# Attention and two expert layers in float32: the first layer's low product moved to GpSimd, the second layer's weights joined during the first layer

## Chip, cores and metric

One core of one Trainium2 chip runs the whole program. The metric is the device time of one execution in microseconds. The kernel before was run three times: 968.38, 967.47 and 964.55 us, median 967.47 us. Most executions of one kernel agree within 0.3%.

## The reference

Three steps follow one another. All inputs arrive as float64 words and the output is float32.

```python
# window attention: batch 4, heads 8, sequence 576, head size 64
scores = scale * q @ k.T + bias            # causal, window of 128, one slope for each head
attn = softmax(scores);  x = (attn @ v) as [2304 tokens, 512]
# first layer: rational activation
h = x @ w_in                               # 512 -> 2048
P = a0 + a1*h + a2*h**2 + a3*h**3;  Q = 1 + |b0|*|h| + |b1|*h**2
x = (P / (Q + 1e-6)) @ w_out               # 2048 -> 512
# second layer: ELU
h = x @ w_in2;  g = where(h > 0, h, exp(min(h, 0)) - 1);  out = g @ w_out2
```

## The kernel before

**Two parts of every operand.** A float32 value is split into a high part that TensorE multiplies exactly and a low part that is the rest. A product is three passes, `PASS` = high by high, low by high, high by low (line 229). So each split costs a copy of the high part, mostly on ScalarE, and a subtraction for the low part, mostly on VectorE.

**Weights arrive as float64.** A weight is two 32-bit words. A scale turns the high word into a float32 (`conv_scale`, line 126), a shift brings down the top bits of the low word (`conv_shift`, line 136), an or and a sign join them (`conv_or`, `conv_sign`), and then `conv_hi` and `conv_lo` split the result. `conv_step` (line 173) moves three weights through these stages at once; in the attention the list `STEPS` places the same stages by hand, one letter each (`s`, `a`, `b`, `c`, `h`, `l`).

**Three stages of the program.** In the attention 16 units of one batch and one pair of heads run in a pipeline whose order is `STEPS`; `normalise` runs on GpSimd. The first layer works on six blocks of 384 tokens. Each block has 16 chunks of 128 hidden columns, 96 chunks in all. For chunk `s` the loop at the end of `experts` issues `gemm1(s)` (12 matmuls, line 248), then `gemm2_T(s - 3)` (12 matmuls, line 691), then `rational(s)`, which holds the activation of chunk `s` and the last operations of chunk `s - 1`. At the end of a block `split_x` splits the next block's input into `xs`. The second layer has 24 steps `q`, eight pairs of hidden chunks for three pairs of token blocks. Each multiplies by a scheme of seven products (`product`, line 887) and then by the second weights (`gemm2`, line 903). The products need sums of weight blocks (`sum_w`, line 830, four operations on GpSimd) and of token blocks (`sum_x`, line 866). A planner, `in_order`, sorts all operations of the second layer by assumed costs and due times.

**Where the second layer's weights are joined.** `load_half`, `join_scale` and `join_words` join 20 of its 32 weights during blocks 1 to 4 of the first layer, in halves of 128x256, and store them in DRAM (`joined`). This happens in ten chunks of each block, 40 halves. The other 12 weights, all of the second matrix, are joined in the second layer by `scale_wo` (ScalarE) and `join_wo` (VectorE, lines 138, 145 and 152).

**Around the change.** Each engine has one queue and works in order. VectorE's order in `rational` is `hi` (line 286), `qq` (288), the join, `qq0` (298), `oo*h` (302), the subtraction (304), the sum (306) and `lo` (308). ScalarE's are the square, `qq`, `oo`, `ee` (lines 273 to 278) and the logarithm and exponential that give the reciprocal `rr` (292, 293). In the last block `prepare` makes the sums and splits for the second layer's first step. `h` lies in PSUM in one of four banks; `h2`, `qq`, `oo`, `ee`, `rr`, `ghi` and `glo` lie in SBUF.

## Time and profile before

| What | us |
|---|---|
| Median of three runs | 967.47 |
| The profiled execution, its own time | 965.85 |
| Its span, first to last instruction | 963.8 |
| TensorE busy (matmul) | 927.3 |
| VectorE busy | 864.8 |
| ScalarE busy | 750.6 |
| GpSimd busy | 232.7 |

The span is 2.05 us shorter than the execution's own time, and that execution lies 1.62 us below the median. Matmuls overlap in the record: one lasts about twice the distance from its start to the next one's start, so TensorE counts as busy when its matmuls follow one another. The attention takes the first 150 us or so, the first layer lasts to about 555 us, and the second layer fills the rest. The mean granted clock of TensorE over the span is 0.991 of 2.4 GHz.

### The profile page before, as it was taken

What the parts mean: (1) busy time and instruction counts of PE and PEld (TensorE: products, weight loads), DVE (VectorE), ACT (ScalarE), POOL (GpSimd) and SP (SyncE); (2) the same over time, 40 slices, a digit from 0 to 9 for tenths busy, and PEclk for the clock granted to TensorE, in tenths of its full rate; (3) what the DMA queues carried; (4) which work ended last, traced back from release to release, by engine and by line L of the source; (5) the groups of instructions that cost most, each with busy time, mean ns of one, the idle gap of its engine ahead of it and who ended that gap; (6) DMA issues with size and microseconds to landing.
All of it is one profiled execution on the core that took longest, in us unless ns stands there. A gap on an engine that the chain in (4) does not pass through costs nothing.

```text
span 963.8 us, 16615 instructions
## 1 busy us (share of the span) xinstructions
PE 927.3 (96%) x5494; PEld 842.7 (87%) x5494; DVE 864.8 (90%) x1949; ACT 750.6 (78%) x1628; POOL 232.7 (24%) x296
## 2 busy tenths in 40 slices
PE   7999999999999999999999979899989999999998
PEld 4776668999999999999999978788978989989897
DVE  5999989999999999999999999999988768887753
ACT  5999999889889888888887967666866657766553
POOL 4777764110000000000000152332254221133100
PEclk9999999999999999999999979999999999999999
DMA  6899842001221212211100124243332221322101
GB/s 169 213 236 247 218 131 82 1 23 33 67 66 50 67 50 66 66 50 60 62 28 1 56 69 129 98 140 113 99 121 86 57 77 56 103 94 78 55 1 66
DMA packets 102486, 83.92 MB, mean 87 GB/s; under 512 B 61696, under 2 KB 83200, under 8 KB 102400
## 3 DMA queue, kind: packets, MB, share of 16 engines
q1 hardware_dynamic: 102400, 82.87, 29.7%
q8 instruction: 43, 0.70, 0.3%
q14 instruction: 43, 0.35, 0.1%
HBM read 69.73 MB, written 13.11 MB: 86 GB/s over the span
## 4 chain that ended last, share of the span: by engine, by line
PE 56%; DVE 20%; ACT 13%; issue 7%; SPq 2%; DMA 1%; DVEq 0%; ACTq 0%
PE acc L691 15%; PE h L248 14%; PE acc L903 14%; PE m L887 12%; ACT pT L427 2%; ACT pr_wo L501 2%; ACT pr_wi L501 2%; DVE qq L288 2%; DVE ghi L286 2%; DVE qq L298 2%; DVE op_wo L847 1%; DVE op_wi L847 1%; DVE oo L302 1%; SPq L334 1%; DVE ee L943 1%
## 5 line engine op out<-in xcount | busy, mean ns | idle before, releaser
L248 PE MATMUL h<-xs,w_wi 128*128 128x384 f32 x1152 | 218.1, 335 | 3.9 <-DVE xs L224 3.4
L248 PEld LDWEIGHTS h<-xs,w_wi 128*128 128x128 f32 x1152 | 200.5, 188 | 6.8 <-DVE xs L224 5.3
L691 PE MATMUL acc<-ghi,w_wo 128*128 128x384 f32 x768 | 196.2, 336 | 0.0
L830 POOL TENSOR_TENSOR s<-two_wo 128x256 f32<-128x256 f32 x32 | 33.3, 1041 | 503.5 <-DMA two_wo<-joined_wi 379.6
L691 PEld LDWEIGHTS acc<-ghi,w_wo 128*128 128x128 f32 x768 | 139.8, 189 | 0.0
L691 PE MATMUL acc<-glo,w_wo 128*128 128x384 f32 x384 | 129.6, 338 | 1.8 <-DVE glo L308 1.8
L887 PE MATMUL m<-xo_wo,op_wi 128*128 128x384 f32 x336 | 79.1, 343 | 12.1 <-DVE ee L943 4.8
L903 PE MATMUL acc<-op_wo,ghi 128*128 128x512 f32 x288 | 89.6, 392 | 0.0
L292 ACT ACTIVATE rr<-qq,c_q 128x384 f32<-128x384 f32 x96 | 59.0, 614 | 27.6 <-DVE qq L288 23.7
L887 PEld LDWEIGHTS m<-xo_wo,op_wi 128*128 128x128 f32 x336 | 60.9, 191 | 20.2 <-DVE ee L943 6.4
L887 PE MATMUL m<-xo_wi,op_wi 128*128 128x384 f32 x336 | 78.2, 341 | 0.0
L691 PEld LDWEIGHTS acc<-glo,w_wo 128*128 128x128 f32 x384 | 72.7, 189 | 3.4 <-DVE glo L308 3.3
L274 ACT ACTIVATE qq<-h,b_abs 128x384 f32<-128x384 f32 x96 | 55.4, 577 | 23.8 <-DVE ee L304 23.8
L275 ACT ACTIVATE oo<-h,a_sb 128x384 f32<-128x384 f32 x96 | 68.0, 708 | 0.7 <-DVE ee L306 0.5
L278 ACT ACTIVATE ee<-h,a_sb 128x384 f32<-128x384 f32 x96 | 67.1, 699 | 0.5 <-DVE glo L308 0.5
L288 DVE SCALAR_TENSOR_TENSOR qq<-h,b_abs,qq 128x384 f32<-128x384 f32 x96 | 60.9, 635 | 5.6 <-ACT qq L274 5.6
L949 ACT ACTIVATE oo<-qq 128x384 f32<-128x384 f32 x24 | 12.6, 525 | 64.7 <-DVE qq L943 64.7
L887 PEld LDWEIGHTS m<-xo_wi,op_wi 128*128 128x128 f32 x336 | 61.4, 190 | 0.0
L903 PEld LDWEIGHTS acc<-op_wo,ghi 128*128 128x128 f32 x288 | 53.5, 188 | 8.9
L903 PE MATMUL acc<-op_wo,glo 128*128 128x512 f32 x144 | 57.0, 396 | 0.0
L943 DVE TENSOR_TENSOR ee<-ee,m 128x384 f32<-128x384 f32 x96 | 52.4, 545 | 4.2 <-PE m L887 4.2
L306 DVE TENSOR_TENSOR ee<-ee,oo 128x384 f32<-128x384 f32 x96 | 54.5, 568 | 0.2
(196 smaller groups left out, 2279.5 us busy)
## 6 DMA issues: line engine op xcount, KB each, us to landing
raw_wo<-in_moe_w_out_dram SPq DMA_DIRECT2D x25, 512.0 KB, 4.8
pair<-joined_wo SPq DMA_DIRECT2D x36, 256.0 KB, 2.7
raw_wi<-in_moe_w_in_dram SPq DMA_DIRECT2D x16, 512.0 KB, 4.3
half<-in_moe_w_in_dram SPq DMA_DIRECT2D x32, 256.0 KB, 2.8
two_wo<-joined_wi SPq DMA_DIRECT2D x32, 256.0 KB, 2.9
v<-in_v_dram SPq DMA_DIRECT2D x32, 128.0 KB, 3.0
joined_wi<-whole SPq DMA_DIRECT2D x32, 128.0 KB, 1.8
two_wi<-joined_wi SPq DMA_DIRECT2D x16, 256.0 KB, 3.0
```

The lines of the kernel that those rows point to most:

```text
L248: nc.tensor.matmul(h, lhsT=WT["wi", f][:, SEL[wp], kk * P:(kk + 1) * P], rhs=x[xp][kk], start=(kk == 0 and n == 0), stop=(kk == KD - 1 and ...
L274: nc.scalar.activation(out=qq, in_=h, func=AF.Abs, scale=b_abs[:, 0:1])
L275: nc.scalar.activation(out=oo, in_=h2, func=AF.Identity, scale=a_sb[:, 3:4], bias=a_sb[:, 1:2])
L278: nc.scalar.activation(out=ee, in_=h2, func=AF.Identity, scale=a_sb[:, 2:3], bias=a_sb[:, 0:1])
L288: nc.vector.scalar_tensor_tensor(out=qq, in0=h2, scalar=b_abs[:, 1:2], in1=qq, op0=ALU.mult, op1=ALU.add)
L292: nc.scalar.activation(out=rr, in_=qq, func=AF.Ln, bias=c_q)
L306: nc.vector.tensor_tensor(out=ee, in0=ee, in1=oo, op=ALU.add)
L501: nc.scalar.activation(out=probs(u, n), in_=probs(u, n), func=AF.Exp, scale=-1.0, bias=mx[:, n:n + 1], accum_out=sm[:, n:n + 1],)
L691: nc.tensor.matmul(acc_t[d], lhsT=WT["wo", f][:, SEL[wp], d * P:(d + 1) * P], rhs=gt[SEL[xp]], start=(f == 0 and n == 0), stop=(f == KF - ...
L887: nc.tensor.matmul(out, lhsT=w[:, SEL[wp], c0:c0 + P], rhs=XO[q // NP2, nm, k][:, SEL[xp]], start=(k == 0 and n == 0), stop=(k == 1 and n ...
L903: nc.tensor.matmul(acc_t[T, t], lhsT=gt[SEL[xp]][:, t * P:(t + 1) * P], rhs=w[:, SEL[wp]], start=(first and n == 0), stop=(last and n == 2),)
L943: nc.vector.tensor_tensor(out=t, in0=R[q, x], in1=M[q, m], op=ALU.add)
```

## The change

Five things change.

1. `top_bits` replaces the shift by a GpSimd operation: it reads the low word as an unsigned number, multiplies by 0.994 times two to the minus 29, subtracts 0.455 and lets the conversion to an integer round. It is used in the attention (`a0`, `a1`), in `conv_step`, and in `join_scale`. In `conv_step` the shift comes one stage earlier, the or, the sign and the low part can be put off into the next `rational`, and the low part goes from GpSimd to VectorE.
2. In `rational`, from chunk 4 on, `h2` lies in PSUM (bank 6), so `gemm1` uses three banks for `h` instead of four. `oo*h` is written over `h` in PSUM and the sum reads it there. The last operation, `low`, goes to GpSimd for chunks over 4. VectorE's order is now `hi`, a first put-off operation, `qq0`, a second one, `qq`, the subtraction, `oo*h`, the sum.
3. 30 of the 32 weights are joined in the first layer, 60 halves in 60 chunks (15 of each of blocks 1 to 4), with scale and shift on GpSimd and or and sign on VectorE.
4. In the last block the preparation is spread, two VectorE operations to a chunk, and takes in one more product's operands (`t1`). The first sums of weights of step 1 go to VectorE. The sums of tokens for the next pair of blocks wait for the products of four later steps, one each.
5. The sums of weights of steps 0 to 7 are stored in DRAM and loaded in steps 8 to 23 instead of being made again.

```diff
+    def top_bits(low):
+        nc.gpsimd.tensor_scalar(
+            out=low, in0=low.bitcast(U32), scalar1=0.994 * 2.0 ** -29, scalar2=-0.455,
+            op0=ALU.mult, op1=ALU.add,
+        )
     def conv_shift(key):
-        low, _ = words(key)
-        nc.vector.tensor_scalar(
-            out=low, in0=low, scalar1=29, scalar2=None, op0=ALU.logical_shift_right
-        )
+        top_bits(words(key)[0])
...
         if new:
             conv_scale(new)
+            conv_shift(new)
         if scaled:
-            conv_shift(scaled)
-            conv_or(scaled)
-            conv_sign(scaled)
+            put_off.append(lambda: conv_or(scaled))
+            put_off.append(lambda: conv_sign(scaled))
         if whole:
-            conv_lo(whole)
+            put_off.append(lambda: conv_lo(whole, "D"))
+        while put_off and not later:
+            go_on()
...
-            h2 = row("h2")
+            h2 = bank(6, [P, TB], "h2") if c > 3 else row("h2")
...
+        one, two = beside or (None, None)
         if old:
...
             nc.vector.tensor_tensor(out=hi, in0=ee0, in1=rr0, op=ALU.mult)
+        if one:
+            one()
+        if old:
+            nc.vector.scalar_tensor_tensor(
+                out=qq0, in0=qq0, scalar=EPSC, in1=hi.bitcast(F32), op0=ALU.add, op1=ALU.mult
+            )
+        if two:
+            two()
         if new:
             nc.vector.scalar_tensor_tensor(
                 out=qq, in0=h2, scalar=b_abs[:, 1:2], in1=qq, op0=ALU.mult, op1=ALU.add
...
         if old:
             nc.vector.tensor_tensor(out=ee0, in0=ee0, in1=qq0, op=ALU.subtract)
+            (nc.gpsimd if c > 4 else nc.vector).tensor_tensor(out=low, in0=ee0, in1=rr0, op=ALU.mult)
         if new:
-            nc.vector.tensor_tensor(out=ee, in0=ee, in1=oo, op=ALU.add)
-        if old:
-            nc.vector.tensor_tensor(out=lo, in0=ee0, in1=rr0, op=ALU.mult)
+            nc.vector.tensor_tensor(out=h, in0=oo, in1=h, op=ALU.mult)
+            nc.vector.tensor_tensor(out=ee, in0=ee, in1=h, op=ALU.add)
...
-        early_ones = [("wi", KF + f) for f in range(KF)] + [("wo", KF + 2 * p) for p in range(4)]
+        early_ones = [("wi", KF + f) for f in range(KF)] + [("wo", KF + f) for f in range(KF - 2)]
...
-            nc.scalar.activation(out=w, in_=high.bitcast(F32), func=AF.Copy, scale=2.0 ** -112)
+            nc.gpsimd.tensor_scalar(
+                out=w, in0=high.bitcast(F32), scalar1=2.0 ** -112, scalar2=1.0, op0=ALU.mult, op1=ALU.mult
+            )
+            top_bits(half[n].rearrange("p (c t) -> p c t", t=2)[:, :, 0])
...
-                step((w, "sum"), "POOL", 2900, lambda: sum_w(w), (w, "load"), (w - 1, "lo", "C"), (w - 1, "lo", "D"))
+                if w >= NP2:
+                    step((w, "sum"), "SP", 1200, lambda: load_sums(w), *gone)
+                else:
+                    eng, cost, at = (nc.vector, 1400, "DVE") if w == 1 else (nc.gpsimd, 3500, "POOL")
+                    step((w, "sum"), at, cost, lambda: sum_w(w, eng), (w, "load"), *gone, (w - 1, "kept"))
+                    step((w, "kept"), "SP", 1200, lambda: keep_sums(w), (w, "sum"))
...
-                step(("sum", J, n), "POOL", 2300, lambda n=n: sum_x(J, n), *used, *[("sum", J, i) for i in range(n)])
+                step(("sum", J, n), "POOL", 2300, lambda n=n: sum_x(J, n), *used, (q - 4 + n, "b11"),
+                     *[("sum", J, i) for i in range(n)])
...
-                run_all(gemm1(s, f, x1[j], 4 + s % 4))
+                run_all(gemm1(s, f, x1[j], (4, 5, 7)[(s - 4) % 3]))
...
+            if s >= LAST:
+                prepare(s)
+            elif s >= KF and f < KF - 1 and nj < 2 * len(early_ones):
+                rational(s, beside=(lambda: join_words(nj), lambda: join_sign(nj)))
```

`keep_sums` issues two stores of 256 KB and `load_sums` two loads of 256 KB.

## Rows read from the trace of the kernel before

**Rows 1.** Busy time by stretch: us, then PE, PEld, DVE, ACT, POOL, clock, DMA, GB/s.
```profile
25.00:128.00 103.00, 98.70 (x990) 73.22 (x988) 101.18 (x395) 102.76 (x324) 78.15 (x120) 1.00 0.87 216
128.00:162.00 34.00, 29.97 (x269) 24.20 (x268) 30.54 (x82) 31.98 (x84) 21.00 (x29) 0.95 0.45 137
162.00:222.00 60.00, 58.53 (x334) 57.34 (x333) 59.45 (x116) 50.78 (x98) 8.01 (x4) 1.00 0.03 10
222.00:537.00 315.00, 312.12 (x1795) 310.76 (x1795) 306.70 (x676) 271.93 (x530) 0.00 (x0) 1.00 0.17 51
...
555.00:575.00 20.00, 14.33 (x58) 13.19 (x58) 19.72 (x30) 11.86 (x24) 11.62 (x10) 0.74 0.11 37
575.00:713.00 138.00, 129.26 (x634) 113.73 (x633) 130.07 (x226) 94.24 (x187) 46.84 (x44) 1.00 0.35 113
713.00:964.00 251.00, 247.30 (x1222) 221.04 (x1220) 184.70 (x332) 157.58 (x314) 50.21 (x52) 1.00 0.23 72
```

**Rows 2.** Waits of TensorE from 128 us on: total us, times, longest us.
```profile
PE m L887 <- DVE ee L943: 6.8, 5, 2.4
PE m L887 <- ACT qq L937: 3.7, 1, 3.7
PE h L248 <- DVE xs L224: 3.4, 5, 0.8
PE m L887 <- DVE qq L943: 3.3, 4, 1.6
PE ps_pT L534 <- ACT pT L427: 3.2, 3, 2.0
PE acc L691 <- DVE glo L308: 1.8, 4, 0.8
```

**Rows 3.** Timeline of TensorE inside the first layer: start, us, what.
```profile
301.27 2.24 PE L248 MATMUL h<-xs,w_wi 128*128 128x384 f32 x12
303.35 0.51 PE L691 MATMUL acc<-ghi,w_wo 128*128 128x384 f32 x2
```

**Rows 4.** Timeline of VectorE, one chunk with a join.
```profile
306.10 0.55 DVE L286 TENSOR_TENSOR ghi<-ee,rr 128x384 fp32r<-128x384 f32 x1
...
307.10 0.28 DVE L764 TENSOR_SCALAR half<-half 128x256 int32<-128x256 int32 x1
...
308.22 0.55 DVE L298 SCALAR_TENSOR_TENSOR qq<-qq,ghi 128x384 f32<-128x384 f32 x1
...
310.56 0.55 DVE L286 TENSOR_TENSOR ghi<-ee,rr 128x384 fp32r<-128x384 f32 x1
```

**Rows 5.** Timelines of GpSimd and VectorE where the second layer begins.
```profile
556.30 7.70 POOL L866 TENSOR_TENSOR xT<-xT 128x384 f32<-128x384 f32 x6
...
560.53 1.35 DVE L298 SCALAR_TENSOR_TENSOR qq<-qq,ghi 128x384 f32<-128x384 f32 x1
```

**Rows 6.** Single lines of the second layer, VectorE: count, min/median/max ns, first and last start.
```profile
L943 DVE TENSOR_TENSOR ee<-ee,m x96: 536/546/555, 571.8 to 950.1; 128x384 f32<-128x384 f32 x96
...
L958 DVE SCALAR_TENSOR_TENSOR oo<-oo,ee x24: 541/557/1101, 585.0 to 951.9; 128x384 f32<-128x384 f32 x24
```

**Rows 7.** Timeline of GpSimd, operations that ran undisturbed.
```profile
24.59 0.47 POOL L518 TENSOR_SCALAR pr_wi<-pr_wi,qq 128x256 f32<-128x256 f32 x1
...
578.07 0.73 POOL L830 TENSOR_TENSOR s<-two_wo 128x256 f32<-128x256 f32 x1 [5.30 <-DVE op_wo L847]
```

**Rows 8.** Timelines of GpSimd and VectorE in one unit of the attention.
```profile
107.47 0.94 POOL L518 TENSOR_SCALAR rr<-rr,qq 128x192 f32<-128x192 f32 x1
107.51 0.69 DVE L152 SCALAR_TENSOR_TENSOR cvt<-raw_wo,cvt 128x512 int32<-128x512 int32 x1
109.55 0.78 POOL L130 TENSOR_SCALAR cvt<-raw_wi 128x512 f32<-128x512 f32 x1 [1.15 <-DVE w_wo L166]
```

**Rows 9.** Joins of second-layer weights on VectorE, count, min/median/max ns, first and last start.
```profile
L138 DVE TENSOR_SCALAR raw_wo<-raw_wo x9: 409/418/423, 587.8 to 673.5; 128x512 int32<-128x512 int32 x9
L145 DVE SCALAR_TENSOR_TENSOR pair<-pair,raw_wo x9: 691/693/696, 588.2 to 674.0; 128x512 int32<-128x512 int32 x9
```

149 lines of the change are left out of this document (86 added, 63 removed).

## The prediction

> **What bounds the kernel now.** I read the busy time by stretch first [rows 1]. TensorE is busy for 312.12 of 315 us in blocks 1 to 5 of the first layer and for 247.30 of 251 us after 713 us. A busy TensorE need not be at its peak, so the timeline decides: 12 matmuls take 303.35 - 301.27 = 2.08 us, 0.173 us each [rows 3], and this distance holds through the stage. The change takes no matmul away. So it can only win what TensorE loses in waits and at the lower clock.
>
> The waits say where that is [rows 2]. After the attention there are 19 of them with 6.8 + 3.7 + 3.4 + 3.3 + 1.8 = 19.0 us. A matmul's record lasts 0.34 us while the next one starts after 0.17 [rows 3], so each wait costs about 0.17 more than its idle time: 22.2 us. Every one but the 3.7 ends with a VectorE operation; that one ends with a ScalarE copy into a buffer that VectorE's subtraction of the last chunks has to free first. In the turn to the second layer, 555 to 575 us, the granted clock is 0.74 on average, so about 10.4 of 20 us ran at 1.2 GHz after TensorE had stood idle; TensorE was busy 14.33/20 = 72% of the time, and half of 7.5 us, 3.7 us, is lost. Around the turn from the attention, 128 to 162 us, three waits cost 3.2 + 0.5 us and the clock of 0.95 costs up to 1.7 us. In all 31 us are within reach, which gives a floor near 935.
>
> VectorE is the engine behind them: 101.18 of 103, 306.70 of 315 and 130.07 of 138 us busy in the attention, the first layer and the early second layer [rows 1]. After 713 us it is busy for 184.70 of 251 us, and TensorE waits for nothing worth a row. So the second layer has no stall where VectorE has a quarter of its time free.
>
> **First layer, VectorE and GpSimd.** A chunk with a join takes VectorE 310.56 - 306.10 = 4.46 us: 1.00 for `hi` and `qq`, 1.12 for three word operations, 2.34 for five more at 0.47 [rows 4]. TensorE needs 24 x 0.173 = 4.16. Ten of sixteen chunks have a join, so the mean is 3.34 + 0.70 = 4.04. Afterwards 15 chunks of a block have one, with 1.00 + two thirds of 1.12 (0.75) + four at 0.47 (1.88) + 0.08, since the sum now depends on the operation just before it and starts at its end, 0.55 rather than 0.47. That is 3.71 us. 0.45 us a chunk is free.
>
> GpSimd gets three operations a chunk. The low product has 384 columns; 256 took 0.73 undisturbed [rows 7], so 1.1. Scale and shift have 256 columns each, 0.47 by the nearest row of one input [rows 7]. The sum is 2.04 of 4.16 us, so GpSimd itself doesn't bind. But the two engines disturb each other. Where GpSimd ran six operations back to back, 1.28 us apart, each VectorE operation with two SBUF inputs took 1.35 us instead of 0.55 [rows 5]. The operations that read one operand from PSUM never grew: 96 sums lie between 536 and 555 ns, while those with two SBUF inputs reach 1101 [rows 6]. After the change three of VectorE's eight operations of a chunk read PSUM: `qq` (0.53 of the 1.00), `oo*h` (0.55) and the sum (0.47).
>
> Now the chunk in order. The subtraction releases the low product; `oo*h` and the sum, 1.02 us, run beside its 1.1, so the next `hi` waits 0.08. Scale and shift follow in GpSimd's queue, and they meet `hi`, an or, `qq0` and a sign, all with two SBUF inputs. A one-input operation that met such a VectorE operation ended 0.21 us after it (107.47 + 0.94 against 107.51 + 0.69), so it needs the shared path for less than half of its time alone [rows 8]. Two such meetings cost 0.42 when neither falls beside `qq`, and 0.21 when one does. So VectorE's chunk takes 3.71 + 0.08 + 0.21 to 0.42 = 4.0 to 4.21 us. Against 4.16 that is nothing, or 0.05 x 60 = 3 us. I take nothing, and keep 3 for the range.
>
> The rounding shift reads an unsigned integer, which no row shows. From below it costs what the scale costs, 0.47; from above I take the two-input operation, 0.73 [rows 7]. The 0.26 more would fall beside `qq` or the subtraction, and at worst 60 x 0.26 = 16 us would come on top. I take the lower end, since the nearest row has the same shape and number of inputs.
>
> Other waits that this adds: the scale waits for the store of the half that used its buffer, and the low product stands behind it in GpSimd's queue. `gemm2_T` reads that low part two chunks later, 8.3 us, against 2.04 us of GpSimd's work, so no loss. ScalarE loses a scale; its `ee` now waits for the low product, which ends before ScalarE needs it. Three banks for `h` instead of four still leave 12.5 us until reuse. One store and one load of a half a chunk instead of in two of three go on SP's queue; the DMA engines were busy 17% of the time there [rows 1].
>
> VectorE's backlog at the block ends shrinks: the five waits for `xs`, 3.4 + 0.8 us, lose 2. The four for `glo`, 1.8 + 0.7 us, belong to conversions and preparation on a full VectorE and to GpSimd at the turn; they lose 1.5. In the last block two extra operations a chunk bring VectorE to about 2.96 + 1.0 to 1.2, about the pace of TensorE, so I give no more.
>
> **The turn to the second layer.** GpSimd's 7.70 us of token sums [rows 5] lengthen the last chunks' operations on VectorE by about 0.8 us each. The change moves these sums to later steps, and the first sums of weights go to VectorE. The copy that TensorE awaits comes some 6 us earlier. The waits of 3.7, 1.6 and 0.3 with their 0.5, and 3.7 for the clock, 9.8 in all, lose 7.5. The rest I leave, because VectorE has two chunks' work still to do when the first product starts.
>
> **Early second layer.** From 575 to 713 us eight waits take 8.5 us (6.8, and 3.3 less 1.6) + 1.4. Ten of twelve joins leave. Each is a shift of 0.42, an or of 0.69 [rows 9] and a sign of 0.69 [rows 8], 18 us of VectorE's 130 us, and brings its share to 112 of 138, or 81%, near the 74% at which nothing waits. These waits lose 8.5 of 9.9. The sums kept in DRAM take 16 x 4 operations from GpSimd, but at a time when TensorE waits for nothing, so I cost them at nothing; the two loads a step stand in SP's queue beside DMA engines busy for 23% [rows 1].
>
> **Attention.** ScalarE is busy for 102.76 of 103 us [rows 1], so VectorE's two shifts less a unit win nothing. GpSimd takes two shifts of 0.78, the price of the strided scale of 512 columns. It stood idle 1.15 us right where they come [rows 8], and (103 - 78.15)/12 = 2.07 us in each of some 12 units [rows 1], against 1.56. In the turn to the first layer VectorE loses shifts of 0.42 [rows 9] and gains low parts of 512 columns, about as long as an or, but GpSimd's low parts, which could block it, go. I take a gain of 1, between -4 and 3.
>
> **The sum.** 1 + 2 + 1.5 + 7.5 + 8.5 = 20.5, with 0.5 for the short restarts behind a wait 21 us. The profiled execution took 965.85 us, so 945; it lies 1.6 us below the median, which I don't add.
>
> **A rule against it.** GpSimd's 1.28 us a turn and VectorE's 1.35 [rows 5] show strict turns, while the 0.21 us [rows 8] shows a shorter hold. The Trainium skill, SBUF — State Buffer, section "SBUF: two separate sides", says that the port pair is locked for a whole instruction by whichever starts first and that the other blocks fully. By that rule 1.35 us agrees, but the 0.21 doesn't show a hold of the whole instruction. What such a hold would do here is the second rival.
>
> **The rivals.**
> 1. The turn stays a stall. VectorE at TensorE's pace in the last block arrives late, `h11` comes after the third product is due, and the clock falls as before; then 7.5 + 1.5 is not won, and 954 results. For it: VectorE is as full there as before. Against: the blocked operations go.
> 2. GpSimd holds the path for its whole time, and the engines take turns. Scale and shift then cost VectorE 0.47 each on top: 3.71 + 0.08 + 0.94 = 4.73 us, 0.57 over TensorE, 60 x 0.57 = 34 us: 979, slower than before. It begins to cost at 0.45 us uncovered a chunk and eats the whole gain at 0.80. A shift of twice its price would do the same. For it: strict turns [rows 5]. Against: the short hold [rows 8].
> 3. GpSimd becomes the attention's bound. With shifts of 1.3 us it would work 2.6 - 2.07 = 0.5 us past its slack in each of 12 units: 6 us, 951.
> 4. The change doesn't do what it says: the joins don't fit and VectorE is relieved in name only. 60 halves fit 60 chunks exactly, so this is unlikely; 965.
>
> **How the numbers follow.** The forecast, 945, has 0.66 (936 to 953); rival 1 has 0.14, rival 2 0.11, rival 3 0.05, rival 4 0.04. The range 936 to 960 takes in the forecast, rivals 1 and 3 and the bounds of the unknown costs. Under 0.5% (about what a measurement of this kernel can tell from no change, 963 to 972) lies rival 4 with the upper edge of rival 1, 0.05; slower has rival 2, 0.11; faster the rest, 0.84.
>
> **What would show it.** Right: matmuls 0.173 us apart all through the first layer, VectorE's operations on PSUM still at 0.55 beside GpSimd's, no clock below 0.95 near 560 us, and no waits for `ee` between 575 and 713. Wrong: waits for `glo` or `h` in blocks 1 to 4 (rival 2), a wait of over 3 us at the third product (rival 1), or GpSimd without gaps in the attention and ScalarE below 0.95 there (rival 3).

## The result and the profile after

| | us |
|---|---|
| Kernel before, median (964.55 to 968.38) | 967.5 |
| Changed kernel, median (976.50 to 980.43) | 978.7 |
| Ratio, with its 95% interval | 1.012, 1.009 to 1.015 |
| Profiled execution of the changed kernel, its own time | 979.0 |
| Its span | 977.3 |

The change made the kernel 1.2% slower. The prediction was 945, faster. The two spans differ by 977.3 - 963.8 = 13.5 us, and the first product of each stage in the two traces tells where they come from:

| Stretch | before, us | after, us | difference |
|---|---|---|---|
| Start to the first `gemm2_T` | 162.61 | 163.27 | +0.7 |
| From there to the first product of block 1 | 53.55 | 55.32 | +1.8 |
| Blocks 1 to 4 | 270.15 | 290.14 | +20.0 |
| Block 5, to the second layer's first product | 68.86 | 68.48 | -0.4 |
| Steps 0 and 1 of the second layer | 41.69 | 38.05 | -3.6 |
| Step 2 to the end | 366.9 | 362.0 | -4.9 |

The second layer won 8.5 us, and blocks 1 to 4, where the joins are, lost 20. Busy time by stretch, with the columns of [rows 1]:

```profile
25.00:128.00 103.00, 94.74 (x979) 72.24 (x977) 96.63 (x366) 101.85 (x319) 97.16 (x141) 1.00 0.86 214
...
218.00:509.00 291.00, 281.21 (x1537) 269.88 (x1538) 270.24 (x522) 214.84 (x420) 142.91 (x185) 0.98 0.26 79
...
577.00:598.00 21.00, 14.36 (x82) 13.74 (x81) 19.88 (x38) 15.00 (x32) 6.43 (x7) 0.92 0.25 89
```

In the second row no engine but TensorE looks full: VectorE is busy for 270 of 291 us, GpSimd for half. Before, VectorE had 306.70 of 315 us there [rows 1]. A stage has become slower although its fullest engine after TensorE became emptier, so I looked for the loss in the order and in the waits. The waits of TensorE from 128 us on, to be laid beside [rows 2]:

```profile
PE h L265 <- ACT xs L240: 10.8, 6, 2.4
PE m L926 <- DVE ee L982: 9.6, 5, 6.5
```

The second row's 6.5 us lie in step 1 of the second layer. Of the first row, five belong to the block ends, 1.7 to 2.4 us each, and behind four of them the granted clock stands at 1.2 GHz for 3.4 us. One chunk with a join in the middle of block 2, VectorE first, GpSimd below (start, us, what; the answer to [rows 4]):

```profile
299.70 0.60 DVE L318 SCALAR_TENSOR_TENSOR qq<-h,b_abs,qq 128x384 f32<-128x384 f32 x1
300.23 0.54 DVE L326 TENSOR_TENSOR ee<-ee,qq 128x384 f32<-128x384 f32 x1
300.69 0.55 DVE L329 TENSOR_TENSOR h<-oo,h 128x384 f32<-128x384 f32 x1
301.34 0.55 DVE L330 TENSOR_TENSOR ee<-ee,h 128x384 f32<-128x384 f32 x1
302.03 0.56 DVE L308 TENSOR_TENSOR ghi<-ee,rr 128x384 fp32r<-128x384 f32 x1
302.50 0.64 DVE L786 SCALAR_TENSOR_TENSOR h<-h,half 128x256 int32<-128x256 int32 x1
303.07 0.77 DVE L312 SCALAR_TENSOR_TENSOR qq<-qq,ghi 128x384 f32<-128x384 f32 x1
303.76 0.41 DVE L794 SCALAR_TENSOR_TENSOR h<-half,h 128x256 int32<-128x256 int32 x1
304.10 0.60 DVE L318 SCALAR_TENSOR_TENSOR qq<-h,b_abs,qq 128x384 f32<-128x384 f32 x1
```
```profile
300.94 1.03 POOL L327 TENSOR_TENSOR glo<-ee,rr 128x384 fp32r<-128x384 f32 x1 [1.91 <-ACT rr L322]
302.05 0.82 POOL L778 TENSOR_SCALAR gwhole<-half 128x256 f32<-128x256 f32 x1
302.95 0.48 POOL L141 TENSOR_SCALAR half<-half 128x256 int32<-128x256 uint32 x1
```

VectorE comes round in 304.10 - 299.70 = 4.40 us, without a wait that the view names, against TensorE's 4.16. Read the distance from each start to the next. Three are longer than their operations need: `hi` starts 0.69 us after the sum, and 0.06 after the low product has ended at 301.97; the or takes 0.57 beside the scale; `qq0` takes 0.69 beside the shift. From this I concluded that each of GpSimd's three operations costs VectorE about 0.22 us. That was the first theory, T.

T is right for the scale and the shift and wrong for the low product. `hi` reads `ee`, which is the result of the sum just before it, and it starts 0.69 us after the sum in e3 too, where GpSimd makes no low product (e1, e3 and e11 are edits told below). e3, VectorE first, GpSimd below:

```profile
311.16 0.56 DVE L330 TENSOR_TENSOR ee<-ee,h 128x384 f32<-128x384 f32 x1
311.85 0.56 DVE L308 TENSOR_TENSOR ghi<-ee,rr 128x384 fp32r<-128x384 f32 x1
```
```profile
310.96 0.42 POOL L778 TENSOR_SCALAR h<-half 128x256 f32<-128x256 f32 x1 [3.57 <-DMA joined_wi<-h]
311.46 0.42 POOL L141 TENSOR_SCALAR half<-half 128x256 int32<-128x256 uint32 x1
```

The median of 76 such pairs in e3 is 0.69 us, as in the changed kernel. In two of e1's 78 pairs `hi` started before the low product had ended, once by 0.22 us, and 0.69 us after its sum all the same. In e11, where `hi` belongs to another chunk than the sum before it and doesn't read its result, the distance is 0.47. So the 0.22 us is the price of reading the result of the operation just before, and of GpSimd's three operations two push VectorE, by 0.23 and 0.22 us.

The block end shows something else. ScalarE there, in the changed kernel and then in the kernel before:

```profile
288.57 0.67 ACT L297 ACTIVATE ee<-h,a_sb 128x384 f32<-128x384 f32 x1
290.47 0.61 ACT L322 ACTIVATE rr<-qq,c_q 128x384 f32<-128x384 f32 x1 [1.23 <-DVE qq L318]
...
291.54 1.75 ACT L240 ACTIVATE xs<-xT 128x384 fp32r<-128x384 f32 x4
```
```profile
280.12 0.70 ACT L278 ACTIVATE ee<-h,a_sb 128x384 f32<-128x384 f32 x1
280.91 0.62 ACT L292 ACTIVATE rr<-qq,c_q 128x384 f32<-128x384 f32 x1
...
281.99 1.75 ACT L223 ACTIVATE xs<-xT 128x384 fp32r<-128x384 f32 x4
```

Before, the logarithm follows `ee` at once. After, it waits 1.23 us for `qq`, since VectorE does `qq` only behind `hi`, the or, `qq0` and the sign. The copies of `xs`, for which TensorE stands idle, queue behind it: that was the second theory, O (order).

### The profile page after: what moved, and what is told of

Its sections match the earlier page's. It is cut to its first block, busy times and chain, and to the rows that moved or that the text cites. A ratio compares the mean times of both kernels' runs of the same rounds, so it can differ in the third digit from the quotient of the medians.

```text
span 977.3 us, 16858 instructions
## 1 busy us (share of the span) xinstructions
PE 935.4 (96%) x5494; PEld 845.9 (87%) x5494; DVE 829.9 (85%) x1805; ACT 720.7 (74%) x1578; POOL 357.1 (37%) x466
## 4 chain that ended last, share of the span: by engine, by line
PE 46%; DVE 35%; ACT 10%; issue 5%; POOL 1%; SPq 1%; DMA 1%; DVEq 0%; POOLq 0%; ACTq 0%
PE acc L942 18%; PE m L926 16%; PE h L265 6%; PE acc L713 5%; DVE qq L312 4%; DVE qq L318 4%; DVE ee L330 3%; DVE ee L326 3%; DVE h L329 3%; DVE ghi L308 2%; DVE cvt L152 2%; DVE cvt L159 1%; DVE gwhole L786 1%; DVE h L786 1%; ACT pr_wi L523 1%
## 5 line engine op out<-in xcount | busy, mean ns | idle before, releaser
L265 PE MATMUL h<-xs,w_wi 128*128 128x384 f32 x1152 | 223.7, 342 | 11.0 <-ACT xs L240 10.8
L265 PEld LDWEIGHTS h<-xs,w_wi 128*128 128x128 f32 x1152 | 204.7, 192 | 15.1 <-ACT xs L240 12.7
L327 POOL TENSOR_TENSOR glo<-ee,rr 128x384 fp32r<-128x384 f32 x92 | 93.6, 1017 | 243.5 <-DVE ee L326 146.5
L713 PE MATMUL acc<-glo,w_wo 128*128 128x384 f32 x384 | 132.7, 346 | 0.8 <-DVE glo L327 0.5
L318 DVE SCALAR_TENSOR_TENSOR qq<-h,b_abs,qq 128x384 f32<-128x384 f32 x96 | 58.4, 608 | 9.5 <-ACT ee L297 9.3
L312 DVE SCALAR_TENSOR_TENSOR qq<-qq,ghi 128x384 f32<-128x384 f32 x96 | 65.0, 677 | 0.5
L297 ACT ACTIVATE ee<-h,a_sb 128x384 f32<-128x384 f32 x96 | 64.5, 672 | 0.0
L294 ACT ACTIVATE oo<-h,a_sb 128x384 f32<-128x384 f32 x96 | 63.9, 666 | 0.0
L308 DVE TENSOR_TENSOR ghi<-ee,rr 128x384 fp32r<-128x384 f32 x96 | 53.7, 559 | 12.0 <-ACT h L292 0.5
L330 DVE TENSOR_TENSOR ee<-ee,h 128x384 f32<-128x384 f32 x96 | 53.2, 554 | 10.1 <-DVE h L329 0.5
```

What stands on the lines that cost most here:

```text
L265: nc.tensor.matmul(h, lhsT=WT["wi", f][:, SEL[wp], kk * P:(kk + 1) * P], rhs=x[xp][kk], start=(kk == 0 and n == 0), stop=(kk == KD - 1 and ...
L294: nc.scalar.activation(out=oo, in_=h2, func=AF.Identity, scale=a_sb[:, 3:4], bias=a_sb[:, 1:2])
L297: nc.scalar.activation(out=ee, in_=h2, func=AF.Identity, scale=a_sb[:, 2:3], bias=a_sb[:, 0:1])
L308: nc.vector.tensor_tensor(out=hi, in0=ee0, in1=rr0, op=ALU.mult)
L312: nc.vector.scalar_tensor_tensor(out=qq0, in0=qq0, scalar=EPSC, in1=hi.bitcast(F32), op0=ALU.add, op1=ALU.mult)
L318: nc.vector.scalar_tensor_tensor(out=qq, in0=h2, scalar=b_abs[:, 1:2], in1=qq, op0=ALU.mult, op1=ALU.add)
```

## The experiments

Every kernel was timed beside the kernel before, whose median was between 966.3 and 967.5. "Chunk" is the median distance between the signs of successive joined chunks on VectorE, "blocks" the time from the first product of block 1 to that of block 5. In the rest of this section every edit is to the changed kernel unless another is named.

| Kernel | time, us | ratio to before, 95% | chunk, us | blocks 1 to 4, us |
|---|---|---|---|---|
| before | 967.5 | | | 270.15 |
| changed | 978.7 | 1.009 to 1.015 | 4.40 | 290.14 |
| e1 scale on ScalarE | 975.4 | 1.008 to 1.013 | 4.35 | 286.24 |
| e2 only low on GpSimd | 974.5 | 1.007 to 1.011 | 4.19 | 285.68 |
| e3 low on VectorE | 1000.5 | 1.033 to 1.038 | 4.55 | 301.09 |
| e4 `oo*h` in SBUF | 1003.6 | 1.037 to 1.040 | 4.65 | 305.29 |
| e7 `qq` first | 1008.9 | 1.041 to 1.046 | 4.62 | 304.95 |
| e9 `xs` early | 977.8 | 1.010 to 1.014 | 4.40 | 287.95 |
| e12 `h2` in SBUF | 971.5 | 1.003 to 1.008 | 4.41 | 285.65 |
| e10 `h2` in SBUF, `qq` first | 958.4 | 0.990 to 0.993 | 4.19 | 275.05 |
| e13 the same, scale on ScalarE | 949.5 | 0.980 to 0.984 | 3.96 | 266.29 |
| e14 the same, two repairs more | 943.5 | 0.974 to 0.978 | 3.96 | 266.74 |

**One GpSimd operation at a time.** Four edits, each against theory T.

```diff
 e1: join_scale
-            nc.gpsimd.tensor_scalar(out=w, in0=high.bitcast(F32), scalar1=2.0 ** -112, ...)
+            nc.scalar.activation(out=w, in_=high.bitcast(F32), func=AF.Copy, scale=2.0 ** -112)
 e2: the same, and
-            top_bits(low)
+            nc.vector.tensor_scalar(out=low, in0=low, scalar1=29, ..., op0=ALU.logical_shift_right)
 e3: rational
-            (nc.gpsimd if c > 4 else nc.vector).tensor_tensor(out=low, ...)
+            nc.vector.tensor_tensor(out=low, ...)
 e4: rational
-            nc.vector.tensor_tensor(out=h, in0=oo, in1=h, op=ALU.mult)
-            nc.vector.tensor_tensor(out=ee, in0=ee, in1=h, op=ALU.add)
+            nc.vector.tensor_tensor(out=oo, in0=oo, in1=h, op=ALU.mult)
+            nc.vector.tensor_tensor(out=ee, in0=ee, in1=oo, op=ALU.add)
```

> The scale of a joined half goes back to ScalarE, so GpSimd has two operations a chunk (the low product and the shift) instead of three. Theory T (taking turns: every GpSimd operation that meets VectorE's two-SBUF operations pushes them by about 0.2 us, which made VectorE's joined chunk 4.40 us against TensorE's 4.16): VectorE's chunk falls by 0.2 us to 4.18, 60 x 0.22 = 13 us and some 1 us a block end come back, 961 to 966. Rival B (three banks of h instead of four and the square in PSUM chain the engines through ScalarE): ScalarE only gets more to do, so nothing comes back, 978 to 985. Rival G (GpSimd's queue is late with the low product and TensorE waits for it): the queue is shorter, a part comes back, 970 to 975, and VectorE's chunk shows idle time.

> Scale back on ScalarE and shift back on VectorE, so that GpSimd keeps only the low product. Theory T: both pushes of about 0.22 us go, and the shift adds 0.33 to 0.42 on VectorE: 4.40 - 0.44 + 0.33 to 0.42 = 4.29 to 4.38, so 60 x 0.02 to 0.11 = 1 to 7 us come back: 972 to 978, slower than with the scale alone moved. Rival B: ScalarE and VectorE both get more, 980 to 1000. Rival G: GpSimd is never late, 960 to 965.

> The low product back on VectorE, as before; scale and shift stay on GpSimd. Theory T: the low product's push of about 0.2 us goes, 0.47 us of its own comes: 4.40 - 0.2 + 0.47 = 4.67, 60 x 0.27 = 16 us slower: 990 to 998. Rival G: TensorE no longer waits for GpSimd, 965 to 975. Rival B: no change from VectorE as long as it has room, 978 to 982.

> The product oo*h is written to SBUF as before, not over h in PSUM, so that the sum behind it has two SBUF inputs while GpSimd makes the low product. Theory T: the sum is now pushed too, where its PSUM input had kept it free; 0.1 to 0.3 us a chunk, 60 x 0.1 to 0.3 = 6 to 18 us slower: 985 to 997. If PSUM operands protect nothing, or if the low product holds up the operation after the sum by the same amount anyway: 978 to 981. Rival B: the bank of h comes free 0.5 us earlier, 965 to 975.

e3 and e4 came out slower, as T said, and farther. e3's chunk took 4.55 us where T said 4.67, and not for T's reason. The low product takes 0.48 to the next start on VectorE. It reads the difference made just before it and starts 0.65 us after that, where 0.47 is usual. The 0.69 ahead of `hi` stays, and the two pushes go, since scale and shift now lie beside operations that read PSUM. e4 shows what an operand in PSUM is worth. With two SBUF inputs the sum took 1.03 us instead of 0.55 beside the low product, and the chunk 4.65 (VectorE, then GpSimd):

```profile
312.87 1.03 DVE L330 TENSOR_TENSOR ee<-ee,oo 128x384 f32<-128x384 f32 x1
```
```profile
312.47 1.01 POOL L327 TENSOR_TENSOR glo<-ee,rr 128x384 fp32r<-128x384 f32 x1 [1.91 <-DVE ee L326]
```

In blocks 1 to 4 both cost about 60 times the difference in chunk, 11 us against 9 and 15 against 15. The rest of their 22 and 25 us lies in the first and the last block and in the second layer.

e1 fell short: 975.4 where T said 961 to 966. Where nothing was in the way, VectorE's chunk did come round in 4.18 to 4.20 us, but one of its waits in blocks 1 to 4 (total us, times, longest us) had grown; in the changed kernel it was 4.4 us in seven times:

```profile
DVE qq L318 <- ACT ee L297: 9.3, 19, 1.5
```

`qq` reads neither `ee` nor anything that this ScalarE operation writes. With the scale on it, ScalarE's own round has become the longer one. e2's time lies in the 972 to 978 that T gave it, but not for T's reason. Nothing pushes VectorE there, and the shift costs it nothing: it stands between the sum and `hi`, 0.47 and 0.22 us to the next starts, the 0.69 of before. The operations alone would make a chunk of 3.98 us. It takes 4.19 because `qq` waits for `ee`: the waits over 0.15 us alone are 26 in blocks 1 to 4, 16.4 us, and its blocks lose as in e1, with 10 us of TensorE's waits for `xs`. So fewer pushes alone don't bring the time back, and O was the next to be tried.

**The order.** e7 moves `qq` to the head of VectorE's chunk; e8 does that with the scale on ScalarE; e9 leaves VectorE alone and issues the copies of `xs`, and `gemm1` of the block's last chunk, ahead of the logarithm.

```diff
 e7: rational
+            if new:
+                nc.vector.scalar_tensor_tensor(out=qq, in0=h2, ...)      # qq of the new chunk
             nc.vector.tensor_tensor(out=hi, in0=ee0, in1=rr0, op=ALU.mult)
 ...
-        if new:
-            nc.vector.scalar_tensor_tensor(out=qq, in0=h2, ...)
 e9: in the last but one chunk of a block
+                run_all(gemm1(s + 1, f + 1, x1[j], ...))
+                return lambda: split_x(j + 1, at_home, nc.vector, "hi")  # ahead of Ln and Exp
```

> One VectorE operation moves: qq of the new chunk (reads PSUM) goes from behind the sign to the head of the chunk, before hi. Everything else is as in the changed kernel, all three GpSimd operations included. Theory T (pushes on the port by turns): behind the release of the low product stand now three operations that read PSUM, 0.65 + 0.55 + 0.55 = 1.75 us, which cover its 1.02 us and a part of the scale; VectorE's chunk falls from 4.40 to 4.0 to 4.2 us, and with it the waits for glo. Theory O (order: since qq stands late, ScalarE's Ln and Exp come late, and the copies of xs for the next block queue behind them; that, and not the chunk's length, is the loss): Ln comes 1.6 us earlier in the chunk, the waits of 2.4 us for xs fall under 1 and the falls of the clock behind them go. Both: 958 to 966. They differ in VectorE's chunk: T 4.0 to 4.2, O 4.4 still, with glo waits left. If neither holds, 976 to 980.

> The same move of qq, and the scale on ScalarE, so that GpSimd has the low product and the shift. T: 1.02 + 0.48 = 1.5 us of GpSimd's work lie under 1.75 us of operations that read PSUM: nothing is pushed, VectorE's chunk is 3.7 to 3.85 us, TensorE sets the pace in the blocks: 954 to 960. O alone: as with the move alone, within 2 us.

> Only ScalarE's four copies of xs for the next block move: they are issued ahead of the Ln and Exp of the block's last but one chunk instead of behind them. O: the waits of 2.4 us and the clock's falls at four or five block ends go, 5 x 2 + 4 x 1.8 = 17 us less: 961 to 966. T: VectorE is still behind at 4.40 us a chunk, so that TensorE waits for glo or for VectorE's part of xs instead; only the clock's falls come back: 970 to 977.

e7 was the surprise: 1008.9 us where both theories said 958 to 966. One round of VectorE, then GpSimd and ScalarE in the same stretch (idle time before and its releaser in brackets):

```profile
333.90 0.62 DVE L301 SCALAR_TENSOR_TENSOR qq<-h,b_abs,qq 128x384 f32<-128x384 f32 x1 [0.80 <-ACT ee L297]
334.44 0.55 DVE L314 TENSOR_TENSOR ghi<-ee,rr 128x384 fp32r<-128x384 f32 x1
334.90 0.42 DVE L791 SCALAR_TENSOR_TENSOR h<-h,half 128x256 int32<-128x256 int32 x1
335.24 0.55 DVE L318 SCALAR_TENSOR_TENSOR qq<-qq,ghi 128x384 f32<-128x384 f32 x1
...
336.04 0.55 DVE L331 TENSOR_TENSOR ee<-ee,qq 128x384 f32<-128x384 f32 x1
336.51 0.55 DVE L334 TENSOR_TENSOR h<-oo,h 128x384 f32<-128x384 f32 x1
...
338.52 0.62 DVE L301 SCALAR_TENSOR_TENSOR qq<-h,b_abs,qq 128x384 f32<-128x384 f32 x1 [0.80 <-ACT ee L297]
```
```profile
336.77 1.02 POOL L332 TENSOR_TENSOR glo<-ee,rr 128x384 fp32r<-128x384 f32 x1 [2.41 <-DVE ee L331]
338.06 0.42 POOL L783 TENSOR_SCALAR h<-half 128x256 f32<-128x256 f32 x1 [0.27 <-DMA joined_wi<-h]
338.55 0.42 POOL L141 TENSOR_SCALAR half<-half 128x256 int32<-128x256 uint32 x1
```
```profile
336.63 0.58 ACT L293 ACTIVATE qq<-h,b_abs 128x384 f32<-128x384 f32 x1 [0.52 <-DVE ee L331]
337.16 0.67 ACT L294 ACTIVATE oo<-h,a_sb 128x384 f32<-128x384 f32 x1
337.82 0.67 ACT L297 ACTIVATE ee<-h,a_sb 128x384 f32<-128x384 f32 x1
```

T is right on the pushes, if partly because VectorE stands idle here: GpSimd's work lies beside that gap and beside operations that read PSUM. Scale and shift take 0.42 us instead of 0.82 and 0.48, no VectorE operation is pushed, `hi` no longer follows the sum, and the distances of its eight operations, with 0.47 for the sum ahead of the gap, add up to 3.74 us. But the round takes 4.62, for `qq` stands 0.03 us behind the end of `ee`. That is no accident of one chunk. In the 92 chunks from chunk 4 on, `qq` never started before `ee` had ended, and in 88 of them it started 0.03 us behind (the expectation of e10, below, has 92 of 96 for that; in the four others of the 92 it started later, by up to 0.15 us); in the kernel before it started before the end of `ee` in 78 of the same 92, by up to 1.16 us. The operand that the two share is `h2`: `oo` and `ee` read it on ScalarE, `qq` on VectorE, and the change put it into PSUM.

That wait closes a ring: the subtraction frees the buffer that `Abs` writes, `Abs`, `oo` and `ee` follow on ScalarE (336.63 to 338.49), then `qq`, `hi`, the or, `qq0`, the sign and the subtraction on VectorE. So theory R: with `h2` in PSUM `qq` can't go first without this ring, and where the change put it, it makes ScalarE late. e8 doesn't tell anything of this. Its scale stood in ScalarE's queue where it waited for the store of the half before it, and everything behind it waited too; one of two such rows of ScalarE's waits in e8:

```profile
ACT gwhole L783 <- DMA joined_wi<-gwhole: 35.7, 15, 3.8
```

It took 1121 us. In e9 the waits for ScalarE's copies of `xs` went, and TensorE waited for VectorE's part of `xs` instead, 8.4 us in 4 waits in blocks 1 to 4. The chunk stayed at 4.40 us and the time at 977.8, just above the 970 to 977 that T gave it; two of the four falls of the clock at the block ends went. A wait was moved, not removed.

**Place and order together.** e12 puts `h2` into SBUF and leaves `qq` where the change has it; e10 does both. e11 keeps `h2` in PSUM, but opens the ring with more buffers. In all three `hi` has three buffers instead of four, in e11 the low part as well.

```diff
 e10 and e12: rational (e10 with the edit of e7 as well)
-            h2 = bank(6, [P, TB], "h2") if c > 3 else row("h2")
+            h2 = row("gh2") if c > 3 else row("h2")
-            hi = row(f"ghi{(c - 1) % 4}", F32R)
+            hi = row(f"ghi{(c - 1) % 3}", F32R)
 e11: rational; VectorE's order is qq, oo*h, sum, hi, or, qq0, sign, subtraction
-            ee = row(f"ee{c % 2}")
-            qq = row(f"qq{c % 2}")
+            ee = row(("ee0", "ee1", "gee2")[c % 3])
+            qq = row(("qq0", "qq1", "gqq2")[c % 3])
...
+            nc.scalar.activation(out=h2, in_=qq, func=AF.Ln, bias=c_q)
+            nc.scalar.activation(out=rr, in_=h2, func=AF.Exp, scale=-1.0)
```

> As the run in which qq stands first, with one thing more: the square h2 lies in SBUF again (two buffers of hi are enough to make room). In that run VectorE's operations of a chunk took only 3.75 us and none was pushed, yet a chunk took 4.6, since qq stood 0.03 us behind the end of ScalarE's ee in 92 of 96 chunks: it waits until ScalarE's two reads of h2's bank in PSUM are done. Theory R (that wait closes a ring sub, Abs, oo, ee, qq, hi, qq0, sub over ScalarE and VectorE): without the bank, qq starts before ee's end as it did before the change, the wait of 69 us goes; but qq is now pushed by GpSimd's low product and scale: VectorE's chunk 4.1 to 4.4 us, 965 to 985. If the ring comes from something else (buffers of qq alone): still 4.6 a chunk, 1000 to 1012.

> The ring opened and the port covered, with all three GpSimd operations kept: VectorE's chunk is qq, oo*h, sum (three reads of PSUM in a row, right behind the subtraction that releases the low product), then hi, or, qq0, sign, sub; qq and ee have three buffers (hi and low three instead of four), and Ln writes over h2 so that it needn't wait for the low product to have read rr. Theory T with R: low, scale and most of the shift lie under 1.75 us of PSUM operations: VectorE 3.8 to 4.0 us a chunk, the ring through ScalarE 3.8, so TensorE sets the pace in the blocks, 67.5 us each: 978.7 - 18 to 22 = 957 to 961. If GpSimd costs VectorE its full push wherever it runs (rival: whole time, strict turns): 4.4 us still, 975 to 985.

> The fourth corner: h2 in SBUF, but qq where the change put it, behind the sign. Theory T with R (the change's late qq has no ring, its chunk of 4.40 us is VectorE's own work with three pushes): h2's place matters little here, and qq with two SBUF inputs is met by nothing of GpSimd's: 975 to 985. If h2's bank alone was the loss, wherever qq stands: 957 to 962.

With e7 these make a square: in PSUM and late 978.7, in PSUM and first 1008.9, in SBUF and late 971.5, in SBUF and first 958.4. Neither move does it alone. Both corners with `h2` in SBUF were faster than I expected, 971.5 against 975 to 985 and 958.4 against 965 to 985. In e12 the chunk is still 4.41 us, for GpSimd pushes as before and `hi` follows the sum. VectorE goes round two of e12's four blocks in 71.3 us without a wait over 0.15 us, where TensorE needs 66.6. So with `qq` late VectorE's own work sets the pace, and the late logarithm of theory O isn't needed to explain it. In e10 the chunk is 4.19 and the kernel is faster than the kernel before. e10's round, with GpSimd's part of it:

```profile
328.92 0.56 DVE L335 TENSOR_TENSOR ee<-ee,h 128x384 f32<-128x384 f32 x1
329.39 0.62 DVE L301 SCALAR_TENSOR_TENSOR qq<-gh,b_abs,qq 128x384 f32<-128x384 f32 x1
329.92 0.78 DVE L314 TENSOR_TENSOR ghi<-ee,rr 128x384 fp32r<-128x384 f32 x1
330.63 0.63 DVE L791 SCALAR_TENSOR_TENSOR h<-h,half 128x256 int32<-128x256 int32 x1
331.18 0.55 DVE L318 SCALAR_TENSOR_TENSOR qq<-qq,ghi 128x384 f32<-128x384 f32 x1
```
```profile
328.52 1.02 POOL L332 TENSOR_TENSOR glo<-ee,rr 128x384 fp32r<-128x384 f32 x1 [1.72 <-DVE ee L331]
329.81 0.48 POOL L783 TENSOR_SCALAR gwhole<-half 128x256 f32<-128x256 f32 x1 [0.27 <-DMA joined_wi<-gwhole]
330.37 0.61 POOL L141 TENSOR_SCALAR half<-half 128x256 int32<-128x256 uint32 x1
```

The low product lies under `oo*h` and the sum and ends 0.15 us into `qq`, which is no longer for it. `hi` takes 0.71 and the or 0.55 to the next start, 0.25 and 0.21 more than in e7. These two pushes are left, `hi` no longer stands behind the sum, and that makes 4.19 us instead of 4.40. `qq` started before `ee` had ended in 89 of 92 chunks. e11's forecast of 957 to 961 was a miss, 967.0. Its chunk was 4.11 us, under TensorE's 4.16, but `qq` still waited for `ee`, and TensorE waited 7.3 us in nine waits for GpSimd's low product. Each block took 69.6 us instead of the 67.5 that I expected. That ScalarE's eight extra copies behind each block end left the round too little room to catch up is my reading, and no run tests it.

**The last push, and the other parts.** e13 takes e10 and puts the scale on ScalarE, between the square and `Abs`, where ScalarE waited for the subtraction. e5 gives the attention's two shifts back to VectorE, in the changed kernel. e6 changes only what the planner assumes of the second layer's start. e14 is e13 with both.

```diff
 e13: rational, and the call with joins (on e10)
             nc.scalar.activation(out=h2, in_=h, func=AF.Square)
+            if between:
+                between()                       # ScalarE's scale of the half that this chunk joins
 e5: the attention's step "a"
-            CONV = {"s": conv_scale, "a": conv_shift, ...}
+            CONV = {"s": conv_scale, "a": conv_shift_v, ...}     # the shift of before, on VectorE
 e6: in_order
-            free = {"PE": 0, "ACT": 1500, "DVE": 2500, "POOL": 0, "SP": 0}
+            free = {"PE": 0, "ACT": 5000, "DVE": 7000, "POOL": 0, "SP": 0}
```

> The kernel with h2 in SBUF and qq first, and the scale on ScalarE, put between Square and Abs, where ScalarE waits 0.8 us a chunk for the subtraction (and where the store that its buffer waits for is two chunks old). Theory T: one push of 0.2 us goes, VectorE's chunk falls from 4.18 to 3.95 to 4.0, under TensorE's 4.16; the blocks' last 5 us over the kernel before (waits for xs) go: 952 to 955. If the remaining 5 us have another cause (ScalarE's chain): 958 to 962.

> Only the two shifts of an attention unit go back to VectorE (in the first conversion of weights; those behind the attention stay on GpSimd). If GpSimd is the attention's bound (97 of 103 us busy, 1.05 us a shift): the unit falls from 8.89 to 8.69 us, the first product of the first layer comes 2 us earlier, and 0.7 to 2.5 us of it reach the end: 976 to 978. If ScalarE still is (102 of 103): no change of the unit, 978.7.

> Only two numbers of the planner change: it is told that ScalarE is free 5.0 us and VectorE 7.0 us after the second layer's first product, instead of 1.5 and 2.5 (in the trace of the changed kernel they are still at the first layer's last chunks until then). If the wait of 6.5 us for the sum h21 in step 1 comes from that order (sums of weights put ahead of it on VectorE): 2 to 6 us and the fall of the clock (3.4 us) go, 970 to 976. If it comes from work that stands there in any order: 977 to 982.

> The same, with the attention's shifts on VectorE and the planner's two start times (5.0 and 7.0 us). If the parts add: 1.5 for the attention and 3.9 for the turn, as each gave alone: 946 to 950, faster than both kernels. If the attention's gain only makes the first blocks wait longer: 949 to 952.

e13 came out at 949.5, better than expected. Its blocks 1 to 4, from the first product of block 1 to that of block 5, have TensorE busy throughout (columns of [rows 1]):

```profile
216.59:482.87 266.28, 266.28 (x1537) 266.23 (x1537) 251.82 (x523) 243.23 (x479) 104.62 (x124) 1.00 0.28 87
```

A block takes 16 x 4.16 = 66.56 us; the kernel before had 67.54. e5 shortened the attention's unit from 8.87 to 8.65 us (ten units between the `x` products at 51.9 and 140.6 us after, at 51.0 and 137.5 in e5); the first `gemm2_T` came 2.8 us earlier, and 1.5 of them reached the end, hardly more than the noise: 977.2. e6 took steps 0 and 1 from 38.05 to 34.46 us, 974.8 in all. e14 is 943.5, 2.4% under the kernel before and 2.5 us under the range that I gave it. An earlier try of several repairs together kept the ring of e7 and shows the same again, 1002.1, so it is only quoted:

> Several repairs at once, to see whether they add: qq first, the xs copies early, the attention's shifts back on VectorE (unit back from 8.89 to 8.69 us, 1.5 to 2.5 us in all), and the planner of the second layer told that ScalarE is free at 5.0 us and VectorE at 7.0 us after the first product (instead of 1.5 and 2.5), which should move the operations that the wait of 6.5 us in step 1 hangs on. T and O: blocks 1 to 4 as before the change (-20), attention -2, turn -3 to -8: 948 to 955.

**What the terms are worth in a kernel that isn't held up.** e15 to e17 take one thing each back from e14: the joins of ten weights, the sums kept in DRAM, and the low product on GpSimd.

```diff
 e15
-        early_ones = [("wi", KF + f) for f in range(KF)] + [("wo", KF + f) for f in range(KF - 2)]
+        early_ones = [("wi", KF + f) for f in range(KF)] + [("wo", KF + 2 * p) for p in range(4)]
 e16
-                if w >= NP2:
+                if False:                       # and no keep_sums
 e17
-            (nc.gpsimd if c > 4 else nc.vector).tensor_tensor(out=low, ...)
+            nc.vector.tensor_tensor(out=low, ...)
```

> The fastest kernel so far (e14), but with the joins of the kernel before: 20 weights of the second layer instead of 30 are joined in the first layer, ten again in the second layer's first steps. My prediction gave those 8.5 us, all of them waits of TensorE between 575 and 713 us: 943.5 + 8.5 = 952. If VectorE's relief there was bought with nothing TensorE waits for: 943 to 945. In the first layer TensorE already sets the pace, so nothing is expected from that side.

> The same (e14), but the sums of the second layer's weights aren't kept in DRAM: GpSimd makes them again in the second half, as before. My prediction costed the kept sums at nothing, since TensorE waits for nothing there: 942.5 to 944.5. If GpSimd's four operations a step push VectorE into TensorE's way, 945 to 950.

> The same (e14), but the low product of the first layer is back on VectorE; GpSimd keeps the shift of a joined half alone. Theory T: in e14 the low product lies under operations that it doesn't push, so all of its 0.47 us come back: VectorE's chunk 3.96 + 0.47 = 4.43 against 4.16, 60 x 0.27 = 16 us and some 2 to 4 us at the block ends: 960 to 965. If GpSimd's low product had cost VectorE as much as it took off: 943 to 947.

e15 took 955.7: the ten early joins are worth 12.2 us. e16 took 943.2: the kept sums are worth nothing, as the prediction had it. e17 took 992.6, 49 us more than e14 where I expected 16 to 22. Its chunk was 4.55 us and not 4.43: the low product reads the difference made just before it and starts 0.58 us after that, where 0.47 is usual. Each of blocks 1 to 4 took 75 us instead of 66.6, 34 us in all. The other 15 lie where I expected nothing, in the first and the last block, whose chunks have the product too, and in the second layer.

## Why the prediction was wrong

**What bounds the kernel** was read rightly. TensorE could win only its waits and the low clock, about 31 us, and VectorE was behind nearly all of them. e14 shows that the amount was there: its span is 941.5, 22.3 us under the kernel before, against my sum of 21. That the two are so close is partly luck, since the shares differ: the joins alone were worth 12.2 us (e15) where I gave 8.5, and the repairs of e14 weren't in my sum.

**First layer, the operations themselves: the term that was mis-sized.** I had 3.71 us a chunk. Without the pushes, 0.23 and 0.22, the changed kernel's 4.40 leaves 3.95. Two of its operations read the result of the one just before them. I counted one of these, the sum, at 0.08 us more than usual; it starts 0.65 us after `oo*h` instead of 0.47, 0.18 more. The other, `hi` behind the sum, I didn't see, and it costs 0.22. The three word operations that became two take 0.07 less than I gave them. e7's 3.74 is so near to 3.71 because `qq` stands between the sum and `hi` there. The room under TensorE's 4.16 was thus about 0.2 us and not 0.45.

**First layer, the pushes.** I had 0.08 for the low product and 0.21 to 0.42 for scale and shift, 4.0 to 4.21 us. The low product cost nothing in the chunk: `hi` is as late behind the sum in e3, without it. Scale and shift cost 0.45 together, just over the upper end of what I gave them, and with the room at 0.2 us that is more than the chunk could hold. The rule of the Trainium skill that I weighed (SBUF — State Buffer, "SBUF: two separate sides", whole-instruction hold by whichever starts first) agrees with the pushes here. The or ended 0.26 to 0.29 us behind the scale's end in 59 chunks of the changed kernel, and `qq0` 0.39 to 0.41 behind the shift's in 57. In e4 the sum ended 0.41 to 0.42 us behind the low product's end in 69 chunks. A push is shorter than GpSimd's own 0.42 us where that operation began first: the shift began 0.12 us ahead of `qq0`.

**First layer, what I didn't see: the place of `h2`.** I counted the operand in PSUM only as shelter for `qq`. It has a price that stands in no duration: all readers of it on another engine. `qq` waits for `oo` and `ee`. In the changed kernel, where it stands late, it never started before the end of `ee` in the 92 chunks; seven waits there took 4.4 us in blocks 1 to 4, e12 has none of them, and its blocks are 4.5 us shorter. At the head of the chunk, e7, the same wait closes the ring. I should have weighed a rule for this. The Trainium skill, PSUM — Partial Sum Buffer, section "PSUM bank collisions raise a hardware error", says that two engines must not be in one bank and quadrant at the same time, reads against reads included, and that the compiler's scheduler therefore adds a dependency between any two such instructions, ScalarE against VectorE too. The trace agrees: never earlier than 0.03 us after `ee`, and with `h2` in SBUF (e10) 89 of 92 earlier. Of the banks the prediction asked only whether three are enough for `h`, not who reads `h2`.

**`xs` and `glo` at the block ends.** I gave them 3.5 us of gain; they became the form that the loss took. With `qq` 1.6 us later in the chunk, the logarithm, the exponential and the copies of `xs` are late, and TensorE waits up to 2.4 us at each block end instead of 0.8 at most [rows 2], with 3.4 us at half the clock behind four of them. e9 shows that these waits are no cause of their own while the chunk is 4.40 us, and e12's blocks, 71.3 us of VectorE's work without a wait, show the cause: VectorE falls behind chunk by chunk, and TensorE pays for it at the block's end.

**The rivals.** Rival 2 (GpSimd holds the path, 979) gave the right time, 978.7, with a chance of 0.11. Its chunk was 4.73 and the measured one 4.40: each push was about half of what it said, and operations that read the result just before them and the rest of each block made up for that. The right time was luck. Against the 266.3 us that blocks 1 to 4 need (e13), an overrun of 0.24 us a chunk cost 23.9 (the changed kernel), 0.39 cost 34 (e17) and 0.49 cost 39 (e4): some 10 us more than 60 times the overrun. I had priced an overrun at 60 chunks and nothing else. About 4 of the 10 are the rest of each block on VectorE, the sixteenth chunk and four subtractions of `xs`: 71.3 - 15 x 4.41 = 5.15 us (e12) against TensorE's 4.16. In e12, whose `qq` hardly waits, these 4 are nearly all: 0.25 a chunk cost 19.4. The changed kernel has the 4.4 us of waits for `ee` besides.

**Attention.** I took a gain of 1, with -4 to 3; it was a loss of 2.4 us at the first product of the first layer (143.75 against 141.36), of which 0.7 was left at the first `gemm2_T`, and rival 3 happened on a small scale. GpSimd is busy for 97.16 of 103 us and the unit grew from 8.62 to 8.87 us. One of GpSimd's two groups for the shift from 25 to 128 us (count, busy us, mean ns, idle time before):

```profile
L141 POOL TENSOR_SCALAR raw_wi<-raw_wi 128x512 int32<-128x512 uint32 x11 | 12.0, 1090 | 0.9
```

I had taken 0.78 for a shift, and it took 1.09 in the mean of this group and 1.03 in that of the other, on `raw_wo`. It isn't the unsigned operand: at 256 columns and undisturbed, e7, shift and scale took 0.42 each. It is the company of VectorE: the shortest of the eleven on `raw_wi` took 0.67.

**The turn.** Of 7.5 us I got 3.6. The three waits of the kernel before went, as forecast, and a new one of 6.5 us came in step 1. The timelines there of VectorE, GpSimd and TensorE, with idle time and its releaser in brackets:

```profile
594.98 1.08 DVE L997 SCALAR_TENSOR_TENSOR oo<-oo,qq 128x384 f32<-128x384 f32 x1
595.98 1.21 DVE L883 TENSOR_TENSOR op_wi<-pair,op_wi 128x512 fp32r<-128x512 f32 x1
597.12 0.54 DVE L982 TENSOR_TENSOR ee<-ee,m 128x384 f32<-128x384 f32 x1
```
```profile
594.54 1.10 POOL L856 TENSOR_TENSOR s<-two_wo 128x256 f32<-128x256 f32 x1 [8.79 <-DVE op_wo L883]
```
```profile
597.80 1.30 PE L926 MATMUL m<-xo_wo,op_wi 128*128 128x384 f32 x3 [6.46 <-DVE ee L982]
```

The sum at 597.12 stands on VectorE behind the sums and splits of weights that the planner put ahead of it, and two of its predecessors are pushed to 1.08 and 1.21 us by GpSimd's four sums from 594.54 on. The planner assumes VectorE free at 2.5 us; with 7.0, and 5.0 for ScalarE instead of 1.5, the wait of 6.5 went, and the longest for that sum was 2.1 (e6). I had written that VectorE has two chunks' work left when the first product starts, and didn't carry it on to the planner's plan.

**Early second layer.** Right in kind, 8.5 forecast. From step 2 to the end the changed kernel won 4.9. The term by itself, e15, is 12.2.

**What I said would show it.** Waits for `glo` or `h` in blocks 1 to 4 were to show rival 2. TensorE's waits there, 9.0 us, were for `xs`, which I hadn't named as a sign, and none of over 0.15 us was for `glo`. GpSimd without gaps and ScalarE below 0.95 were to show rival 3: GpSimd was busy for 97.16 of 103 us, but so was ScalarE for 101.85. No wait for `ee` was to be left in the early second layer; 9.6 us were. VectorE's operations on PSUM kept their 0.55 us, as forecast. At the first product of the second layer the clock held, as forecast; it fell behind the new wait in step 1.

## What to carry to other kernels

Before an operand is moved to PSUM, list every engine that touches its bank: the readers take turns, and a chain through two engines that had slack can close into a ring. Where one engine's round is within 10% of the bound, write the round out start to start with each release, each meeting on the shared path and each operation that reads the result just before it, and write it for the whole block, not for one chunk alone. A distance that is too long can have two reasons, here a neighbour's work or the operand; a kernel without the neighbour (e3) tells them apart. An operation that doesn't need the result, put between the two, is nearly free (`qq` in e10, the shift in e2). A change with a fault in one stage can hide gains in others; here 1.2% slower became 2.4% faster by moving one tile and one operation, one scale, two shifts and two numbers of the planner.
